# A sigmoid gate's logits and exponential in a gated mix of sliding-window attention and a GEGLU layer

## The chip, the cores and the metric

The kernel runs on one core of a Trainium2 chip. The time is device microseconds (us) of one execution. The median of 7 runs of the kernel before is 740.52 us, the lowest 739.31 and the highest 741.72. Engines are named as in the profile: PE is TensorE (matmuls), PEld its weight loads, DVE is VectorE, ACT is ScalarE, POOL is GpSimd, SP is SyncE, which issues most of the DMAs here.

## What is computed

With x of 2048 rows by 1024 columns, the output is `g * a + (1 - g) * b`, where

```
g = sigmoid((x * gate_w).sum(-1, keepdims=True))      # one number per row
a = attention(x @ wqkv) @ wo                          # 32 heads of 32, window of 8 keys, dilation 2
b = (gelu(x @ w_gate) * (x @ w_up)) @ w_down          # 1024 -> 3584 -> 1024
```

The attention of a row looks at the keys 0, 2, 4 ... 14 rows back, with a softmax over the 8. Everything stored is bfloat16.

## The kernel before

**Tiling.** The 2048 rows are worked on as four chunks of 512 rows (`SC`), two chunks forming a "super" step (`sup`). x stands transposed in `xr`, two chunks at a time, eight tiles of 128 columns (`KT`) per chunk; `xT(c, kt)` is one such tile, 128 by 512. The projections q, k, v of chunks 0 and 1 are plain products (`qkv`, `qkv_outer`, matmuls at L469). Those of chunks 2 and 3 (`qkv_pair`, L585), the GEGLU layer (`ffn`, L952) and the output products (`down`, L1096) use a Strassen scheme with seven block products. Its sums of blocks ("forms") are made on DVE: of x in `x_forms` (L449 to L454, called T1, T2, T3, T4 below, in the order of the code), of the q, k, v weights in `qkv_forms` (L552), of the GEGLU weights in `wforms` (L430). T3 is made in place over a tile of x, so it waits for the gate's matmuls of the even chunk (key `("z", c0)`) to have read that tile.

**Attention** is done on DVE and ACT alone, in halves of 256 rows: `scores` (products and sums, L765, L771), then `att_half`: transposes (L828), folds (L835, L838), maximum (L851), subtraction (L858), the exponential on ACT (L863), sums, the reciprocal (L869), the multiplication by the gate (L871), and the weighting of v (L904 to L921).

**The gate.** `gate(c)` multiplies chunk c's eight x tiles with the gate vector `gcol`. It uses the 128x128 array as four column tiles of 32: the eight tiles go in two rounds of four, each round's four matmuls to different groups of 32 output partitions (L693). The output bank thus holds four partial sums in four groups of 32 equal rows. DVE transposes the bank in blocks of 32 (L699) and copies the 16 columns that matter into `zq` (L703). Later `gate_sum(c)` adds the four partial sums with four small float32 matmuls against the 0/1 matrix `qsum` (L717), and DVE clamps the result to +-80 into `zc` (L721). `gate_exp(c)` takes the exponential on ACT into `ez` (L728), and `gate_tail(c)` makes `1/(1+ez)` on DVE in `omg` (L737 to L740). The output products are scaled by `omg` when they leave PSUM; the attention weights are multiplied by `ez`.

**Order.** Eight generators (`main`, `loads`, `wforms`, `x_forms`, `qkv_forms`, `preps`, `attention`, `scores`) yield operations with an engine, a cost in us and dependencies. The planner `Weave.run` holds the head of each generator and always emits the one whose planned start plus the generator's bias is smallest (0.0 for `main` and `loads`, 0.1 for the forms, 0.3 for `attention`, 0.5 for `scores`). The emitted order is final for each engine; the chip follows it and waits where data are not there. A changed cost in the planner can therefore change the order on any engine. Within one generator the order is that of the code. `gate(0)` is issued after chunk 0's projections, `gate_sum(0)` in chunk 1's, `gate(1)` before the first GEGLU, `gate_sum(1)` two steps into it. `gate(2)` and `gate(3)` come after the first output products and before `qkv_pair(2)`, with both sums behind it. `gate_exp(c)` comes in the attention stream, after the subtraction of the chunk's first half and before its exponential, but waits only for `zc`. An ACT operation has a table name; where it differs from the last one (exponential or gelu), the planner adds 1.29 us, and the chip runs an ACT_TABLE_LOAD.

**Setup.** `ident`, the identity for the transposes of x, lies in a corner of `hT`, a large tile that later takes other data. `qsum` is built on POOL with a memset and four affine selects.

Of the kernel before, what the change touches and what calls it, by code (L numbers as in the profile page):

```python
# [8 lines left out]
ACT = mybir.ActivationFunctionType  # L9
ALU = mybir.AluOpType  # L10
BF16 = mybir.dt.bfloat16
F32 = mybir.dt.float32
AP = bass.AP

P = 128
# [4 lines left out]
SC = 512  # L20
NST = SC // P
# [3 lines left out]
ZMAX = 80.0  # L25
# [111 lines left out]
def kernel(  # L137
# [12 lines left out]
    nc = tc.nc  # L150
    Bsz, S, D = A_x.shape
    Df = B_w_gate.shape[1]
    x = A_x.rearrange("b s d -> (b s) d")
    o2 = out.rearrange("b s d -> (b s) d")
    assert Bsz == 1
    KT = D // P
# [18 lines left out]
    scale = float(DH) ** -0.5  # L175
# [3 lines left out]
    consts = ctx.enter_context(tc.tile_pool(name="consts", bufs=1))  # L179
    persist = ctx.enter_context(tc.tile_pool(name="persist", bufs=1))  # L180
    work = ctx.enter_context(tc.tile_pool(name="work", bufs=2))
    small = ctx.enter_context(tc.tile_pool(name="small", bufs=1))
# [8 lines left out]
    hT = persist.tile([P, 2 * NST, FT, P], BF16)  # L191
# [7 lines left out]
    banks = [psum.tile([P, SC], F32, name=f"ps{i}") for i in range(8)]  # L199
    xbuf = persist.tile([P, NB, NWIN * AC], BF16)  # L200
    gcol = consts.tile([P, KT], BF16)
    ident = hT[:, NST + 1, 0, :]
    w = Weave(nc, tc)
    n = NWIN * AC
    V = nc.vector.tensor_tensor
# [1 line left out]
    def xT(c, kt):  # L207
        return xr[:, 2 * (c % 2) + kt // KH, kt % KH, :]

    def hflat(j, f0, n):  # L210
        return hT[:, j, f0:f0 + n, :].rearrange("p f s -> p (f s)")
# [4 lines left out]
    def dve(cost, fn, deps=(), **kw):  # L216
        return Op("DVE", cost, fn, deps, **kw)

    def act(cost, fn, deps=(), **kw):
        return Op("ACT", cost, fn, deps, **kw)  # L220

    def pe(n, fn, deps=(), **kw):
        return Op("PE", n * MM, fn, deps, tail=0.17, **kw)
# [3 lines left out]
    def bank_take():  # L227
        best = min(range(len(bank_free)), key=lambda i: -1.0 if bank_free[i][1] is None else bank_free[i][1].end)
        return bank_free.pop(best)

    def bank_give(i, op):
        bank_free.append((i, op))
# [41 lines left out]
        nc.tensor.matmul(banks[7][:], lhsT=warm[:, 0:P], rhs=warm, start=True, stop=True)  # L274
    wj = consts.tile([P, 1], F32)
    nc.scalar.activation(out=wj[:], in_=warm[:, 0:1], func=ACT.Exp)
    make_identity(nc, ident)
    qsum = consts.tile([P, 32], F32)
    nc.gpsimd.memset(qsum[:], 0.0)
    for d in range(-P + 32, 1, 32):  # L280
        nc.gpsimd.affine_select(out=qsum[:], in_=qsum[:], compare_op=ALU.not_equal, fill=1.0, base=d,
                                pattern=[[-1, 32]], channel_multiplier=1)
    nc.vector.memset(kT[0][:, :, 0:HALO], 0.0)
    nc.vector.memset(vT[0][:, :, 0:HALO], 0.0)
    with nc.allow_non_contiguous_dma(reason="gate vector, one element per partition"):
# [170 lines left out]
    gates = {}  # L456
# [227 lines left out]

    def gate(c):
        i, free = bank_take()
        dx = [("x", c, kt) for kt in range(KT)] if c else []

        def go():
            for r in range(KT // 4):  # L690
                for q in range(4):
                    kt = 4 * r + q
                    nc.tensor.matmul(banks[i][32 * q:32 * (q + 1), :], lhsT=gcol[:, kt:kt + 1].to_broadcast([P, 32]),  # L693
                                     rhs=xT(c, kt), start=(r == 0), stop=(r == KT // 4 - 1),
                                     tile_position=(0, 32 * q), skip_group_check=True)
        o = pe(KT // 4 + 1, go, ([free] if free else []) + dx, key=("z", c))
        yield o
        zt = work.tile([P, SC], F32, tag="u2", bufs=2, name="zt")
        e = dve(0.63, lambda: nc.vector.transpose(out=zt[:], in_=banks[i][:]), [o])  # L699
        yield e  # L700
        bank_give(i, e)
        zq = small.tile([P, SC // 32], F32, tag="zq", bufs=2, name="zq")
        e = dve(0.1, lambda: nc.vector.tensor_copy(out=zq[:], in_=zt[:].rearrange("p (b j) -> p b j", j=32)[:, :, 0]), [e],  # L703
                key=("zq", c))
        yield e
        zc = small.tile([P, SC // 32], F32, tag="zc", bufs=2, name="zc")
        ez = small.tile([P, SC // 32], F32, tag="ez", bufs=2, name="ez")
        omg = small.tile([P, NST], F32, tag="omg", bufs=3, name="omg")
        gates[c] = (ez, omg, zc, zq)

    def gate_sum(c):
        i, free = bank_take()
        zc, zq = gates[c][2:]

        def go():
            for q in range(4):
                nc.tensor.matmul(banks[i][32 * q:32 * (q + 1), 0:SC // 32], lhsT=qsum[:], rhs=zq[:], start=True, stop=True,  # L717
                                 tile_position=(0, 32 * q), skip_group_check=True)
        o = pe(1, go, [("zq", c)] + ([free] if free else []))
        yield o  # L720
        e = dve(0.1, lambda: nc.vector.tensor_scalar(out=zc[:], in0=banks[i][:, 0:SC // 32], scalar1=ZMAX, scalar2=-ZMAX,  # L721
                                                     op0=ALU.min, op1=ALU.max), [o], key=("zc", c))
        yield e
        bank_give(i, e)

    def gate_exp(c):
        ez, zc = gates[c][0], gates[c][2]
        e = act(0.1, lambda: nc.scalar.activation(out=ez[:], in_=zc[:], func=ACT.Exp), [("zc", c)], table="exp", lag=1.0,  # L728
                key=("ez", c))
        yield e  # L730

    def gate_tail(c):
        ez, omg = gates[c][:2]

        def tail():
            og = small.tile([P, SC // 32], F32, tag="og", name="og")
            nc.vector.tensor_scalar(out=og[:], in0=ez[:], scalar1=1.0, scalar2=1.0, op0=ALU.mult, op1=ALU.add)  # L737
            nc.vector.reciprocal(out=og[:], in_=og[:])
            for q in range(4):
                nc.vector.tensor_copy(out=omg[32 * q:32 * (q + 1), :],  # L740
                                      in_=og[32 * q:32 * (q + 1), :].rearrange("p (j q) -> p j q", q=4)[:, :, q])
        yield dve(1.2, tail, [("ez", c)], lag=0.6, key=("omg", c))
# [59 lines left out]
    def att_half(c, a, h):  # L802
# [13 lines left out]
        def lsb():  # L816
            return flat("z").bitcast(F32)[:, 0:CW].rearrange("p (w c) -> p w c", w=NWIN)
# [40 lines left out]
        o = dve(tt(CW, True), lambda: V(out=lsb(), in0=lsb(), in1=m4()[:, 0:1, :].to_broadcast([P, NWIN, CB]),  # L858
                                        op=ALU.subtract), [o])
        yield o  # L860
        if a == 0:
            yield from gate_exp(c)
        e = act(0.55, lambda: nc.scalar.activation(out=lsb(), in_=lsb(), func=ACT.Exp, scale=scale), [o], table="exp",  # L863
                lag=0.6)
        yield e
        if a == 0:
            yield from gate_tail(c)
# [74 lines left out]
            if t + 2 == NT:  # L942
                xb_give(box["ab"], ms[t + 1])

    def ffn(sup, mid, early=()):
        T3, B22, B11, B21 = xr[:, 0], xr[:, 1], xr[:, 2], xr[:, 3]
        T1, T2, T4 = tf[:, 0], tf[:, 1], tf[:, 2]

# [26 lines left out]
        for i in range(FT + 2):  # L975
# [6 lines left out]
                yield ev[f, "seed"]  # L982
            while late:
                yield late.pop(0)
            if i == 1:
                for g in early:
                    yield from g
            if i >= FT:
                yield from mid[i - FT]
            if i >= 2:  # L990
# [191 lines left out]
    def main():  # L1182
        ne = 0
        for j in range(NST):
            for k0 in range(0, KT, KH):
                i, free = bank_take()
                pt = banks[i][:].bitcast(BF16)[:, 0:KH * P].rearrange("p (k s) -> p k s", k=KH)

                def go(pt=pt, j=j, k0=k0):
                    for kk in range(KH):  # L1190
                        nc.tensor.transpose(out=pt[:, kk, :], in_=hflat(j, k0 + kk, 1), identity=ident)
                o = Op("PE", 0.3, go, [free] if free else [], tail=0.17)
                yield o
                dst = xr[:, k0 // KH, :, j * P:(j + 1) * P]
                if ne % 2:
                    e = act(0.48, lambda pt=pt, dst=dst: nc.scalar.copy(out=dst, in_=pt), [o], key=("pt", j, k0 // KH))
                else:
                    e = dve(0.34, lambda pt=pt, dst=dst: nc.vector.tensor_copy(out=dst, in_=pt), [o],
                            key=("pt", j, k0 // KH))
                yield e  # L1200
                bank_give(i, e)
                ne += 1
        yield from qkv_outer(0)
        yield from qkv(0, 1)
        yield from qkv(0, 2)
        yield from gate(0)
        yield from halo(1)
        for which in range(3):
            yield from qkv(1, which)
            if which == 0:  # L1210
                yield from gate_sum(0)
        yield from gate(1)
        for sup in range(NSUP):
            c0 = 2 * sup
            more = sup + 1 < NSUP
            parts = down(c0)
            yield from ffn(sup, parts, [gate_sum(1)] if sup == 0 else [])
            yield from parts[2]
            if more:
                yield from halo(c0 + 2)  # L1220
                yield from gate(c0 + 2)
                yield from gate(c0 + 3)
                yield from qkv_pair(c0 + 2)
                yield from gate_sum(c0 + 2)
                yield from gate_sum(c0 + 3)
                yield from halo(c0 + 3)
            for part in down(c0 + 1):
                yield from part
            if more:
                yield from q_move(c0 + 3)  # L1230
# [33 lines left out]
```

## Time and profile before

| what | value |
|---|---|
| median of the runs | 740.52 us |
| the profiled execution's own time | 741.35 us |
| its span on the core | 739.6 us |
| mean granted PE clock | 0.992 |
| PE busy | 721.5 us (98%) |
| DVE busy | 631.2 us (85%) |
| ACT busy | 312.5 us (42%) |
| L693, gate matmuls | 32, in four groups of 8 |
| L717, matmuls of the partial sums | 32 records, 8 per chunk |
| L728, gate exponentials | 4, 0.22 us each |
| ACT_TABLE_LOAD | 11 in all, 1.283 us each |

The span is what the profiler saw of the core; the execution's own time is 1.75 us longer. A matmul's duration in a group (379 ns) is its passage through the array; in a dense stretch matmuls start every 0.219 us (49 in 10.74 us). Sums of PE durations are therefore no measure of PE's time; gaps and the chain are.

### The profile page before, as it was taken

How to read it: one execution, taken by the hardware profiler on the slowest of the kernel's cores; microseconds unless marked ns; L12 is line 12 of the kernel's file. 1: busy time of each engine (PE TensorE's matmuls, PEld its weight loads, DVE VectorE, ACT ScalarE, POOL GpSimd, SP SyncE). 2: the span in 40 equal slices, each digit the busy share in tenths (PEclk: the TensorE clock that was granted, in tenths of full speed). 3: DMA queues.
4: the chain of work that ended last, by engine and by line, in shares of the span. 5: the costliest groups of instructions: out<-in, count | busy, mean ns of one | idle time of the engine just before them, and what ended most of it. 6: DMA issues, size and time to landing. Idle time of an engine off the chain costs nothing.

```text
span 739.6 us, 9888 instructions
## 1 busy us (share of the span) xinstructions
PE 721.5 (98%) x3330; PEld 355.7 (48%) x3397; DVE 631.2 (85%) x935; ACT 312.5 (42%) x530; POOL 72.0 (10%) x128
## 2 busy tenths in 40 slices
PE   8999999999999999969999999999999999999997
PEld 5666644444444444425665444444444444444443
DVE  2689999999999999996999999989999999896300
ACT  2333455558555542015444122585558554310110
POOL 2234422121111000000000001000000000001000
PEclk9999999999999999979999999999999999999999
DMA  8999955555646469960235999746464645899992
GB/s 306 316 326 361 388 195 178 163 179 164 196 146 205 158 197 323 318 224 28 86 115 167 313 310 319 242 144 172 129 178 133 172 138 162 275 308 326 335 302 103
DMA packets 150435, 162.68 MB, mean 220 GB/s; under 512 B 22896, under 2 KB 110960, under 8 KB 150384
## 3 DMA queue, kind: packets, MB, share of 16 engines
q1 hardware_dynamic: 141552, 134.25, 59.0%
q0 software_dynamic: 8544, 27.27, 10.1%
q8 instruction: 26, 0.43, 0.3%
q10 hardware_dynamic: 288, 0.52, 0.2%
q14 instruction: 25, 0.20, 0.1%
HBM read 129.50 MB, written 28.31 MB: 213 GB/s over the span
## 4 chain that ended last, share of the span: by engine, by line
PE 92%; DMA 6%; issue 1%; DVE 1%; SPq 0%; ACT 0%; DVEq 0%
PE ps L952 46%; PE ps L1096 27%; PE ps L585 10%; PE ps L469 9%; DMA ring<-in_A_wqkv_dram 3%; DMA ring<-oforms 1%; DMA ring<-in_A_wo_dram 1%; DMA hT<-in_B_w_down_dram 1%; SPq L302 0%; DVE zt L699 0%; DVE tf L451 0%; DVE tf L449 0%; PE ps L693 0%; SPq L270 0%; DVE ring L552 0%
## 5 line engine op out<-in xcount | busy, mean ns | idle before, releaser
L952 PEld LDWEIGHTS <-ring 128*128 128x128 bf16 x1568 | 153.2, 98 | 185.0 <-issue 0.4
L952 PE MATMUL ps<-xr,ring 128*128 128x512 bf16 x878 | 210.4, 379 | 0.9
L952 PE MATMUL ps<-tf,ring 128*128 128x512 bf16 x658 | 162.6, 379 | 0.8
L1096 PE MATMUL ps<-ring,hT 128*128 128x512 bf16 x693 | 159.7, 379 | 0.8
L1096 PEld LDWEIGHTS <-hT 128*128 128x128 bf16 x708 | 69.2, 98 | 83.4
L765 DVE TENSOR_TENSOR xbuf<-qo,kT 128x2048 bf16<-128x2048 bf16 x64 | 77.4, 1217 | 2.9 <-ACT kT L491 2.9
L904 DVE TENSOR_TENSOR xbuf<-xbuf,vT 128x2048 bf16<-128x2048 bf16 x64 | 77.3, 1216 | 0.1
L771 DVE TENSOR_TENSOR xbuf<-xbuf 128x2048 bf16<-128x2048 bf16 x56 | 68.1, 1216 | 0.1
L585 PEld LDWEIGHTS <-ring 128*128 128x128 bf16 x336 | 44.1, 132 | 39.2 <-DVE ring L552 9.7
L1131 ACT ACTIVATE ost<-ps,omg 128x512 bf16<-128x512 f32 x16 | 11.0, 687 | 113.4 <-PE ps L1096 110.2
L469 PE MATMUL ps<-xr,ring 128*128 128x512 bf16 x250 | 55.7, 380 | 0.9 <-DMA ring<-in_A_wqkv_dram 0.6
L1024 ACT ACTIVATE gl<-ps 128x512 bf16<-128x512 f32 x56 | 33.5, 597 | 51.7 <-PE ps L952 51.2
L981 ACT COPY ps<-ps 128x512 f32<-128x512 f32 x56 | 32.0, 571 | 55.1 <-PE ps L952 54.9
L1123 POOL DMA_DIRECT2D out_dram<-ost x24 | 13.0, 540 | 433.9 <-ACT ost L1131 340.2
L1096 PE MATMUL ps<-ring,qo 128*128 128x512 bf16 x187 | 49.0, 379 | 1.0 <-DMA ring<-in_A_wo_dram 0.5
L469 PEld LDWEIGHTS <-ring 128*128 128x128 bf16 x256 | 36.4, 144 | 19.7 <-DMA ring<-in_A_wqkv_dram 1.4
L996 DVE TENSOR_TENSOR hT<-hT,gl 128x1024 bf16<-128x1024 bf16 x56 | 38.4, 685 | 8.7 <-ACT hT L993 7.6
L585 PE MATMUL ps<-xr,ring 128*128 128x512 bf16 x187 | 43.0, 379 | 0.4 <-issue 0.2
L585 PE MATMUL ps<-tf,ring 128*128 128x512 bf16 x142 | 36.2, 403 | 7.3 <-DVE ring L552 7.2
L1036 DVE TENSOR_TENSOR u<-ps,u 128x512 f32<-128x512 f32 x56 | 38.3, 685 | 5.3 <-PE ps L952 4.3
L912 DVE TENSOR_TENSOR xbuf<-xbuf 128x1024 bf16<-128x1024 bf16 x64 | 41.9, 685 | 0.6
L438 POOL DMA_DIRECT2D fforms<-ring x56 | 30.5, 544 | 119.7 <-DVE ring L430 116.5
(106 smaller groups left out, 727.1 us busy)
## 6 DMA issues: line engine op xcount, KB each, us to landing
ring<-dforms SPq DMA_DIRECT2D x112, 256.0 KB, 4.8
ring<-in_B_w_down_dram SPq DMA_DIRECT2D x84, 256.0 KB, 4.3
ring<-in_B_w_gate_dram SPq DMA_DIRECT2D x56, 256.0 KB, 5.1
fforms<-ring POOLq DMA_DIRECT2D x56, 256.0 KB, 4.4
ring<-fforms SPq DMA_DIRECT2D x56, 256.0 KB, 3.9
ring<-in_B_w_up_dram SPq DMA_DIRECT2D x42, 256.0 KB, 3.7
ring<-in_A_wqkv_dram SPq DMA_DIRECT2D x40, 256.0 KB, 5.9
ring<-oforms SPq DMA_DIRECT2D x32, 256.0 KB, 5.6
```

The lines of the kernel that those rows point to most:

```text
L469: nc.tensor.matmul(banks[bk][:], lhsT=lhsT, rhs=xT(c, kt), start=(kt == 0), stop=(kt == KT - 1))
L585: nc.tensor.matmul(banks[bk][:], lhsT=lhsT, rhs=rhs[:, kt, :], start=(start and kt == 0), stop=(kt == KH - 1), skip_group_check=True)
L765: V(out=w3(box[t]), in0=q_b, in1=k_w, op=ALU.mult)
L771: V(out=w3(box[0]), in0=w3(box[0]), in1=w3(box[t]), op=ALU.add)
L904: return dve(tt(n), taking(("p", t), lambda: V(out=w3(box["p", t]), in0=w3(box["ab"]), in1=v_w, op=ALU.mult)), [("qkv", c, 2, t), abo] + ( ...
L912: V(out=s4(t)[:, t % 2], in0=w3(box["p", t])[:, 0:4], in1=w3(box["p", t])[:, 4:8], op=ALU.add)
L952: nc.tensor.matmul(banks[bk][:], lhsT=wv[:, k, fl * P:(fl + 1) * P], rhs=rhs[:, k, :], start=(start and k == 0), stop=(k == KH - 1), skip_ ...
L981: ev[f, "seed"] = act(0.5, lambda f=f: nc.scalar.copy(out=banks[Bk[f]][:], in_=banks[A[f]][:]), [o, fr] if fr else [o])
L996: yield dve(tt(2 * SC), lambda f=f: nc.vector.tensor_tensor(out=hT[:, :, f, :], in0=hT[:, :, f, :], in1=gl[f][:].rearrange("p (j s) -> p j ...
L1024: nc.scalar.activation(out=gl[f][:, SC:2 * SC], in_=banks[A[f]][:], func=ACT.Gelu_apprx_tanh)
L1036: e = dve(tt(SC, True), lambda f=f: nc.vector.tensor_tensor(out=u2[f][:], in0=banks[Dk[f]][:], in1=u2[f][:], op=ALU.add), [o, ev[f, "u2"]])
L1096: nc.tensor.matmul(banks[bk][:], lhsT=l, rhs=wv[:, i, :], start=(start and k == 0), stop=(q == last and i == 1), skip_group_check=True)
```

## The change

The gate goes through the full array: eight matmuls per chunk, each with the gate vector broadcast over all 128 columns, accumulate into one bank, which then holds the finished sum in all rows. `qsum`, `zq` and `gate_sum` are gone, with the hook in `ffn` and the calls in `main`; DVE clamps `zt` straight into `zc`, inside `gate`. `gate_exp` is gone too: where a chunk's first half takes its exponential, one ACT operation issues the gate's exponential and the attention's, one behind the other; it waits for both the subtraction and `zc`. `ident` gets a tile of its own. The planner's cost of `gate` goes from 3 matmul times to 8; the operation of the two exponentials costs 0.65 in place of 0.1 and 0.55, and the gate's own `lag` of 1.0 is gone.

```diff
-    ident = hT[:, NST + 1, 0, :]
+    ident = consts.tile([P, P], BF16)
...
-    qsum = consts.tile([P, 32], F32)
-    nc.gpsimd.memset(qsum[:], 0.0)
-    for d in range(-P + 32, 1, 32):
-        nc.gpsimd.affine_select(out=qsum[:], in_=qsum[:], compare_op=ALU.not_equal, fill=1.0, base=d,
-                                pattern=[[-1, 32]], channel_multiplier=1)
...
     def gate(c):
         i, free = bank_take()
         def go():
-            for r in range(KT // 4):
-                for q in range(4):
-                    kt = 4 * r + q
-                    nc.tensor.matmul(banks[i][32 * q:32 * (q + 1), :], lhsT=gcol[:, kt:kt + 1].to_broadcast([P, 32]),
-                                     rhs=xT(c, kt), start=(r == 0), stop=(r == KT // 4 - 1),
-                                     tile_position=(0, 32 * q), skip_group_check=True)
-        o = pe(KT // 4 + 1, go, ([free] if free else []) + dx, key=("z", c))
+            for kt in range(KT):
+                nc.tensor.matmul(banks[i][:], lhsT=gcol[:, kt:kt + 1].to_broadcast([P, P]), rhs=xT(c, kt),
+                                 start=(kt == 0), stop=(kt == KT - 1))
+        o = pe(KT, go, ([free] if free else []) + ([("x", c, kt) for kt in range(KT)] if c else []), key=("z", c))
         yield o
         zt = work.tile([P, SC], F32, tag="u2", bufs=2, name="zt")
         e = dve(0.63, lambda: nc.vector.transpose(out=zt[:], in_=banks[i][:]), [o])
         yield e
         bank_give(i, e)
-        zq = small.tile([P, SC // 32], F32, tag="zq", bufs=2, name="zq")
-        e = dve(0.1, lambda: nc.vector.tensor_copy(out=zq[:], in_=...), [e], key=("zq", c))
-        yield e
+        yield dve(0.1, lambda: nc.vector.tensor_scalar(out=zc[:], in0=..., scalar1=ZMAX, scalar2=-ZMAX, ...), key=("zc", c))
...
-    def gate_sum(c):
-        ...
-    def gate_exp(c):
-        ez, zc = gates[c][0], gates[c][2]
-        e = act(0.1, lambda: nc.scalar.activation(out=ez[:], in_=zc[:], func=ACT.Exp), [("zc", c)], table="exp", lag=1.0,
-                key=("ez", c))
-        yield e
...
-        if a == 0:
-            yield from gate_exp(c)
-        e = act(0.55, lambda: nc.scalar.activation(out=lsb(), in_=lsb(), func=ACT.Exp, scale=scale), [o], table="exp",
-                lag=0.6)
+        def exps():
+            if a == 0:
+                nc.scalar.activation(out=gates[c][0][:], in_=gates[c][2][:], func=ACT.Exp)
+            nc.scalar.activation(out=lsb(), in_=lsb(), func=ACT.Exp, scale=scale)
+        e = act(0.65 if a == 0 else 0.55, exps, [o] + ([("zc", c)] if a == 0 else []), table="exp", lag=0.6,
+                key=("ez", c) if a == 0 else None)
         yield e
```

More of the change, by code (lines that the diff above doesn't have):

```diff
@@ L276 @@
     nc.scalar.activation(out=wj[:], in_=warm[:, 0:1], func=ACT.Exp)
-    make_identity(nc, ident)
-    qsum = consts.tile([P, 32], F32)
-    nc.gpsimd.memset(qsum[:], 0.0)
-    for d in range(-P + 32, 1, 32):
-        nc.gpsimd.affine_select(out=qsum[:], in_=qsum[:], compare_op=ALU.not_equal, fill=1.0, base=d,
-                                pattern=[[-1, 32]], channel_multiplier=1)
+    make_identity(nc, ident[:])
     nc.vector.memset(kT[0][:, :, 0:HALO], 0.0)
@@ L686, in gate @@
         i, free = bank_take()
-        dx = [("x", c, kt) for kt in range(KT)] if c else []
         def go():
-            for r in range(KT // 4):
-                for q in range(4):
-                    kt = 4 * r + q
-                    nc.tensor.matmul(banks[i][32 * q:32 * (q + 1), :], lhsT=gcol[:, kt:kt + 1].to_broadcast([P, 32]),
-                                     rhs=xT(c, kt), start=(r == 0), stop=(r == KT // 4 - 1),
-                                     tile_position=(0, 32 * q), skip_group_check=True)
-        o = pe(KT // 4 + 1, go, ([free] if free else []) + dx, key=("z", c))
+            for kt in range(KT):
+                nc.tensor.matmul(banks[i][:], lhsT=gcol[:, kt:kt + 1].to_broadcast([P, P]), rhs=xT(c, kt),
+                                 start=(kt == 0), stop=(kt == KT - 1))
+        o = pe(KT, go, ([free] if free else []) + ([("x", c, kt) for kt in range(KT)] if c else []), key=("z", c))
         yield o
@@ L701, in gate @@
         bank_give(i, e)
-        zq = small.tile([P, SC // 32], F32, tag="zq", bufs=2, name="zq")
-        e = dve(0.1, lambda: nc.vector.tensor_copy(out=zq[:], in_=zt[:].rearrange("p (b j) -> p b j", j=32)[:, :, 0]), [e],
-                key=("zq", c))
-        yield e
         zc = small.tile([P, SC // 32], F32, tag="zc", bufs=2, name="zc")
+        yield dve(0.1, lambda: nc.vector.tensor_scalar(out=zc[:], in0=zt[:].rearrange("p (b j) -> p b j", j=32)[:, :, 0],
+                                                       scalar1=ZMAX, scalar2=-ZMAX, op0=ALU.min, op1=ALU.max),
+                  key=("zc", c))
         ez = small.tile([P, SC // 32], F32, tag="ez", bufs=2, name="ez")
         omg = small.tile([P, NST], F32, tag="omg", bufs=3, name="omg")
-        gates[c] = (ez, omg, zc, zq)
-    def gate_sum(c):
[L712 to L722, printed above, removed]
-        yield e
-        bank_give(i, e)
-    def gate_exp(c):
-        ez, zc = gates[c][0], gates[c][2]
-        e = act(0.1, lambda: nc.scalar.activation(out=ez[:], in_=zc[:], func=ACT.Exp), [("zc", c)], table="exp", lag=1.0,
-                key=("ez", c))
-        yield e
+        gates[c] = (ez, omg, zc)
     def gate_tail(c):
-        ez, omg = gates[c][:2]
+        ez, omg, zc = gates[c]
         def tail():
@@ L943, in att_half, with ffn @@
                 xb_give(box["ab"], ms[t + 1])
-    def ffn(sup, mid, early=()):
+    def ffn(sup, mid):
         T3, B22, B11, B21 = xr[:, 0], xr[:, 1], xr[:, 2], xr[:, 3]
@@ L984, in ffn @@
                 yield late.pop(0)
-            if i == 1:
-                for g in early:
-                    yield from g
             if i >= FT:
@@ L1190, in go @@
                     for kk in range(KH):
-                        nc.tensor.transpose(out=pt[:, kk, :], in_=hflat(j, k0 + kk, 1), identity=ident)
+                        nc.tensor.transpose(out=pt[:, kk, :], in_=hflat(j, k0 + kk, 1), identity=ident[:])
                 o = Op("PE", 0.3, go, [free] if free else [], tail=0.17)
@@ L1209, in main @@
             yield from qkv(1, which)
-            if which == 0:
-                yield from gate_sum(0)
         yield from gate(1)
@@ L1216, in main @@
             parts = down(c0)
-            yield from ffn(sup, parts, [gate_sum(1)] if sup == 0 else [])
+            yield from ffn(sup, parts)
             yield from parts[2]
@@ L1223, in main @@
                 yield from qkv_pair(c0 + 2)
-                yield from gate_sum(c0 + 2)
-                yield from gate_sum(c0 + 3)
                 yield from halo(c0 + 3)
```

## The prediction

> **What bounds the kernel now.** I read the page's slices first, then the chain of waits, then the timelines where the chain leaves PE. The slices:
>
> ```profile
> PE   8999999999999999969999999999999999999997
> PEclk9999999999999999979999999999999999999999
> ```
>
> PE is full from slice 1 on but for slice 17, and only there does its clock fall. The chain shows that the gate lies in the full parts:
>
> ```profile
> 50.32 0.55 PE ps L693 x8
> ...
> 64.76 0.26 PE ps L717 x8
> ...
> 92.80 0.55 PE ps L693 x8
> ...
> 98.64 0.19 PE ps L717 x8
> ...
> 103.94 10.74 PE ps L952 x49
> ...
> 403.06 0.25 PE ps L717 x16
> ```
>
> Columns are start, length, what. Chunk 0's and 1's gates (L693) and all partial sums (L717) stand between matmuls that follow without a gap; 49 matmuls in 10.74 us make 0.2192 us each. The gates of chunks 2 and 3 are not on the chain. PE's timeline around the hole of slice 17:
>
> ```profile
> 318.72 1.05 PE L693 MATMUL ps<-xr,gcol 128*32 128x512 bf16 x16
> 319.97 1.67 PE L585 MATMUL ps<-xr,ring 128*128 128x512 bf16 x7 [0.21 <-issue]
> 323.19 0.41 PE L585 MATMUL ps<-tf,ring 128*128 128x512 bf16 x1 [1.54 <-DVE ring L552]
> 325.26 0.62 PE L585 MATMUL ps<-tf,ring 128*128 128x512 bf16 x1 [1.66 <-DVE ring L552]
> 329.82 5.89 PE L585 MATMUL ps<-tf,ring 128*128 128x512 bf16 x14 [3.95 <-DVE ring L552]
> ```
>
> After both gates PE has one burst, then idles 1.54 + 1.66 + 3.95 = 7.15 us for weight forms of L552. The last row has 14 matmuls in 5.7 us: windows of 1 us show a granted clock of 0.50 from 326 to 335. At full clock they take 14 x 0.2192 = 3.07, so the slow clock costs 2.7 us. DVE meanwhile (five of its rows):
>
> ```profile
> 319.37 2.31 DVE L828 STREAM_TRANSPOSE xbuf<-xbuf 128x2048 bf16<-128x2048 bf16 x1
> 321.61 1.18 DVE L449 TENSOR_TENSOR tf<-xr 128x2048 bf16<-128x2048 bf16 x1
> ...
> 325.72 0.71 DVE L699 STREAM_TRANSPOSE zt<-ps 128x512 f32<-128x512 f32 x1
> ...
> 327.54 0.70 DVE L699 STREAM_TRANSPOSE zt<-ps 128x512 f32<-128x512 f32 x1
> ...
> 329.35 4.78 DVE L552 TENSOR_TENSOR ring<-ring 128x512 bf16<-128x512 bf16 x14
> ```
>
> DVE never rests there: attention, four x forms, the gates' transposes, and only then the forms that PE wants. So one price list holds where PE is full and another in the hole.
>
> **The change part by part.**
>
> Gates of chunks 0 and 1: each goes from 0.55 us to 8 x 0.2192 = 1.75, +1.20, and nothing hides it: 2 x 1.20 = +2.41.
>
> Partial sums of chunks 0 and 1: 0.26 + 0.19 = 0.45 us leave the full part; those of 2 and 3, 0.25 more, leave at 403. Sum -0.70.
>
> Does the +1.96 before the hole reach its end? DVE sets that end, and DVE is held to PE: in the GEGLU stage L1036 waited for PE 16 times (4.3 us) and L1015 18 times (3.9 us), the last such wait being 0.48 us at 260.5. From there DVE works densely to 329. A later PE moves that anchor, and so the hole's end. I take the whole 1.96; the lower end is 0, if DVE had slack unseen.
>
> Gates of chunks 2 and 3: also +2.41 on PE, but ahead of 7.15 us of idling. The first burst would end near 324 instead of 321.6 on the old axis, and the form it meets is at 323.2. I take 0. The cover gone, they cost +2.41. Below nothing: the planner sees these gates 5 matmul times later each (1.08), and may put forms ahead of the transposes and T3. If the 14 forms of L552 went first, where T3 (L453) starts now at 326.35, the 3.95 us wait would shrink by 3.0 (329.35 less 326.35) and the slow clock's 2.7 could go with it: -5.7. The nearest rows are those of today's order, so I keep 0.
>
> The slow clock stays in my sum, since the 3.95 us wait is still there. The Trainium skill ("TensorE: Matmul & The Clock Gate", Part 1) says that the clock falls to half after an idle window of some 3.4 us, windows running free of the kernel. The row agrees in kind: the fall came about 325, after 3.2 us of broken idling since 321.6. By the rule a gate that fills 2.4 us of the idling could put the fall off, for -2.7 at most; with a wait of 3.95 still whole it should fall anyway.
>
> DVE: a gate loses the copy L703 (0.16) and the clamp L721 (0.17) and gains a clamp from SBUF, put at 0.16 by L703. In the hole one replaces the other: 0. The clamps at 403 lie beside dense PE: 0.
>
> ACT: the gate's exponential (0.22) moves from before to beside the attention's. What the step waits for is late already: the subtraction L858. Chunk 3 is the case in the middle of the GEGLU, where gelus have to wait for a table:
>
> ```profile
> 556.87 1.28 ACT L728 ACT_TABLE_LOAD   x1
> 558.17 0.22 ACT L728 ACTIVATE ez<-zc 128x16 f32<-128x16 f32 x1
> ...
> 559.38 0.63 ACT L863 ACTIVATE xbuf<-xbuf 128x512 f32<-128x512 f32 x1
> 560.03 1.28 ACT L1040 ACT_TABLE_LOAD   x1
> ...
> 562.33 0.59 ACT L1006 COPY m<-ps 128x512 f32<-128x512 f32 x1
> ```
>
> Merged, load and both exponentials are one block of 1.28 + 0.22 + 0.63 = 2.1 us at about 559.4. Queued behind it are a gelu L1040, L993 and the copy L1006, for which PE waits before the block's fourth product. L1006 normally starts at 554.53 plus the step of 6.04, 560.57; here it ended at 562.92, and PE wanted it near 563.15: the gelu L1024 started at 556.26 on its product's end, the next product ends four matmuls later at 557.1, and one step on that is 563.15. So 0.24 us are left; 1.5 us more (the load and the exponential shifted behind it) would stall PE by 1.2. The plain block at 172.28 (load, exponential, then L1006 ended 174.69, wanted near 174.95) passed with 0.26 to spare, and the merged step adds 0.22. I take 0, with ends 0 and +1.2.
>
> Tables: no load disappears, since each gate exponential already shares its load with the attention's (261.85 and 556.87) or finds it there (74.32). The Trainium skill ("ScalarE: Activation LUTs", Table sets) advises to do calls of one set together, at an estimated 2.66 us for each switch saved. By it the sum would be 2.66 lower if one were saved; the eleven loads give no candidate.
>
> POOL and SP: five POOL instructions for `qsum` (0.12 and 1.06 us, done by 3.75 us) stand behind the identity and before nothing that PE awaits: 0. They uncover at most 1.2 at the start, where DMA leads the chain until 24. No DMA is added. Loads that were put down to L717 (SP waited 0.5 and 0.4) find the matmul before it instead. A bank is held 1.2 us longer by a gate and not taken by a sum: 0. `ident` on its own: 0, as the load into its old place waits for the same transposes of x.
>
> Sum: 2.41 - 0.45 - 0.25 = +1.71. Against the profiled execution: 741.35 + 1.71 = 743.06. That one stands 0.83 above the median, 740.52, from which I forecast 742.2.
>
> **The rivals.**
>
> The hole shrinks. For it: the gates' transposes and T4 stand before the awaited L552, and both come later in the plan. Against it: these generators have the smaller bias or come first in a tie. At its price, 740.52 + 1.71 - 5.7 = 736.5. This is the other side; it decides once the hole loses 3.2 us (1.71 + 1.48).
>
> The early gates are hidden. If DVE runs free of PE before the hole, only -0.25 is left: 740.3. For it: DVE dense from 271 to 334. Against: its waits for PE until 260.5.
>
> The hole or ACT grows. If both late gates come out in full, 1.71 + 2.41: 744.6; the stall of 1.2 on top gives 745.8. For it: 0.24 us of slack at L1006, and free planner time before later transposes that attention operations (bias 0.3) can fill, L828 with its 2.3 us above all.
>
> That the change doesn't do what it says: exponentials that are not adjacent. It would show on ACT and move nothing by itself.
>
> **How the numbers follow.** A measurement of this kernel tells about 0.2%, 1.48 us: slower is above 742.0, faster below 739.04. The forecast has 0.45, the growing hole or ACT stall 0.23, the shrinking hole 0.20, the hidden gates 0.12. The growing case is slower throughout; the forecast lies 0.2 over the bound, but its open ends (ACT's 1.2, part of 2.41) point upward: 0.37 slower and 0.08 same. The shrinking case I put at 0.18 faster and 0.02 same, the hidden gates at 0.02 faster and 0.10 same. That makes slower 0.60, same 0.20, faster 0.20. The range takes the priced ends, 736.5 to 745.8; the forecast's own is 741.4 to 743.4 (a third of the late gates' 2.41 less, or the stall of 1.2 more).
>
> **What would show it.** Right: L693 as two pieces of 1.75 us at about 50 and 94 on the chain, no L717; the GEGLU's first matmul at 95.5 for 93.34 (two gates more, one sum of 0.26 less: +2.15); sixteen gate matmuls in 3.5 us near 321; waits for L552 of some 5 us, the clock at 0.5 for some 10 us; eleven table loads. Wrong: another order of L828, L699, L453, L454 and L552 on DVE around 320 to 333, or a gap on PE before the L952 that waits for L1006 near 563. An order changed elsewhere, where no gap is today, would only add.

## The result and the profile after

The changed kernel takes 742.78 us (median of 16 runs, 741.52 to 743.93), the kernel before 740.53 (38 runs). The ratio is 1.0029, with a 95% interval of 1.0021 to 1.0036: 2.25 us slower, where 1.71 were forecast (742.2). The first profiled execution of the changed kernel took 741.72 us, 1.06 under its median; a second one (run e12 below) took 743.54. Both are used here, since they differ in two places that the change has nothing to do with. All ratios leave out runs that lie far above the others of the same kernel; that concerned one run, of 1557.78 us, in e7.

The slices of the changed kernel's page, then its chain at the same places as before (start, length, what):

```profile
PE   8999999999999999969999999999999999999997
PEclk9999999999999999989999999999999999999999
```

```profile
49.55 1.73 PE ps L685 x8
...
92.72 1.73 PE ps L685 x8
...
97.31 10.82 PE ps L923 x49
```

The line numbers have moved: L685 is the gate, L923 the GEGLU, L464 the first projections, L580 and L547 the later ones and their weight forms, L1064 the output products, L797 the attention's transpose (before: L693, L952, L469, L585, L552, L1096, L828). The early gates are 1.73 us each for 0.55, still in the full part; the partial sums are gone. The hole of slice 17 on PE, and some of DVE's rows beside it:

```profile
319.11 3.62 PE L685 MATMUL ps<-xr,gcol 128*128 128x512 bf16 x16
322.56 1.89 PE L580 MATMUL ps<-xr,ring 128*128 128x512 bf16 x8
324.29 0.38 PE L580 MATMUL ps<-tf,ring 128*128 128x512 bf16 x1
326.04 0.41 PE L580 MATMUL ps<-tf,ring 128*128 128x512 bf16 x1 [1.37 <-DVE ring L547]
327.53 0.41 PE L580 MATMUL ps<-tf,ring 128*128 128x512 bf16 x1 [1.08 <-DVE ring L547]
332.21 4.12 PE L580 MATMUL ps<-tf,ring 128*128 128x512 bf16 x12 [4.27 <-DVE ring L547]
```

```profile
320.16 2.31 DVE L797 STREAM_TRANSPOSE xbuf<-xbuf 128x2048 bf16<-128x2048 bf16 x1
322.39 1.18 DVE L444 TENSOR_TENSOR tf<-xr 128x2048 bf16<-128x2048 bf16 x1
...
326.62 0.42 DVE L820 TENSOR_TENSOR xbuf<-xbuf 128x256 f32<-128x256 f32 x1
327.05 0.43 DVE L547 TENSOR_TENSOR ring<-ring 128x512 bf16<-128x512 bf16 x1
327.39 0.71 DVE L690 STREAM_TRANSPOSE zt<-ps 128x512 f32<-128x512 f32 x1
...
331.32 4.44 DVE L547 TENSOR_TENSOR ring<-ring 128x512 bf16<-128x512 bf16 x13
```

The last wait is shorter than this row says. The trace lacks the record of the first matmul behind it; its weight load is there:

```profile
331.80 0.15 PEld L580 LDWEIGHTS <-ring 128*128 128x128 bf16 x2 [4.16 <-DVE ring L547]
```

In the kernel before, and in e5, the first weight load behind the wait and its matmul start within 0.01 us of each other, so the long wait ends at 331.80 and lasts 3.86 us, not 4.27. The second execution (e12) lacks the same record: its wait ends at 332.77, not 333.18, and lasts 3.86 us too. The numbers below use the weight loads here. PE's waits for forms are then 6.3 us for 7.15; the 2.4 us that the late gates got longer have filled idle time. But the long wait ends at 331.80 for 329.82, of which 0.8 us is the later start of the output products. On DVE the gates' transposes have moved behind one attention operation (L820) and one more weight form (L547), as the planner now thinks the gates later.

Cut at six moments that exist in every kernel here, the timelines give these stretches (us; "long wait" is the last wait for the weight forms, and its end the start of the matmuls behind it):

| stretch | before | after | e12 | e3 | e5 | e10 |
|---|---|---|---|---|---|---|
| start to first gate | 50.25 | 49.38 | 50.42 | 49.43 | 50.27 | 49.55 |
| to second gate | 42.47 | 43.17 | 43.16 | 43.16 | 43.17 | 42.48 |
| to first output product | 167.49 | 168.44 | 168.36 | 168.54 | 168.36 | 167.91 |
| to end of long wait | 69.61 | 70.81 | 70.83 | 69.08 | 70.83 | 69.64 |
| to second output products | 73.42 | 71.70 | 72.58 | 72.54 | 70.17 | 70.85 |
| to last matmuls | 331.53 | 331.62 | 331.62 | 331.61 | 331.62 | 331.54 |

The second row is the same within 0.01 us in all executions of one kind of gate. By the second and third rows the early gates and sums cost 0.70 + 0.87 = 1.6 us (e12 against before). The third row varies more: e10, which does the same work as the kernel before up to there, has 167.91, 0.28 of it a wait for ACT, and against it the cost would be 1.15. The fourth row is DVE's: 1.2 us more. The fifth gives back 0.84 (e12) to 1.7 (after). The first row moves by 1 us between two executions of one kernel (49.38 and 50.42).

### The profile page after: what moved, and what is told of

It is laid out like the page before. It is cut to its first block, busy times and chain, and to the rows that moved or that the text cites. A ratio compares the mean times of both kernels' runs of the same rounds, so it can differ in the third digit from the quotient of the medians.

```text
span 739.9 us, 9811 instructions
## 1 busy us (share of the span) xinstructions
PE 722.9 (98%) x3298; PEld 358.0 (48%) x3365; DVE 631.1 (85%) x931; ACT 312.3 (42%) x530; POOL 71.2 (10%) x123
## 4 chain that ended last, share of the span: by engine, by line
PE 92%; DMA 4%; DVE 2%; issue 1%; ACT 0%; ACTq 0%
PE ps L923 45%; PE ps L1064 25%; PE ps L464 11%; PE ps L580 10%; DMA ring<-oforms 1%; DMA ring<-in_A_wo_dram 1%; DMA ring<-in_A_wqkv_dram 1%; DMA ring<-fforms 1%; DMA ring<-dforms 1%; DMA hT<-in_A_x_dram 0%; PE ps L685 0%; DVE hT L1032 0%; PE ps L1159 0%; DVE tf L1032 0%; DVE ring L547 0%
## 5 line engine op out<-in xcount | busy, mean ns | idle before, releaser
L923 PEld LDWEIGHTS <-ring 128*128 128x128 bf16 x1568 | 153.4, 98 | 185.2 <-issue 0.4
L923 PE MATMUL ps<-xr,ring 128*128 128x512 bf16 x878 | 210.4, 379 | 0.8
L923 PE MATMUL ps<-tf,ring 128*128 128x512 bf16 x659 | 162.6, 379 | 0.8
L1064 PE MATMUL ps<-ring,hT 128*128 128x512 bf16 x693 | 159.4, 379 | 0.7
L1064 PEld LDWEIGHTS <-hT 128*128 128x128 bf16 x708 | 69.3, 98 | 83.5
L580 PEld LDWEIGHTS <-ring 128*128 128x128 bf16 x336 | 44.0, 131 | 37.0 <-DVE ring L547 8.5
L464 PE MATMUL ps<-xr,ring 128*128 128x512 bf16 x250 | 55.3, 379 | 0.6 <-DVE xr L1166 0.3
L952 ACT COPY ps<-ps 128x512 f32<-128x512 f32 x56 | 32.0, 572 | 55.7 <-PE ps L923 55.6
L1064 PE MATMUL ps<-ring,qo 128*128 128x512 bf16 x189 | 49.1, 379 | 1.0 <-DMA ring<-in_A_wo_dram 0.4
L464 PEld LDWEIGHTS <-ring 128*128 128x128 bf16 x256 | 36.7, 143 | 18.8 <-DMA ring<-in_A_wqkv_dram 0.3
L580 PE MATMUL ps<-xr,ring 128*128 128x512 bf16 x188 | 43.2, 379 | 0.3
L983 DVE TENSOR_TENSOR hT<-ps,m 128x512 bf16<-128x512 f32 x56 | 38.4, 686 | 4.2 <-PE ps L923 3.9
```

The lines of the kernel that those rows point to most:

```text
L464: nc.tensor.matmul(banks[bk][:], lhsT=lhsT, rhs=xT(c, kt), start=(kt == 0), stop=(kt == KT - 1))
L580: nc.tensor.matmul(banks[bk][:], lhsT=lhsT, rhs=rhs[:, kt, :], start=(start and kt == 0), stop=(kt == KH - 1), skip_group_check=True)
L923: nc.tensor.matmul(banks[bk][:], lhsT=wv[:, k, fl * P:(fl + 1) * P], rhs=rhs[:, k, :], start=(start and k == 0), stop=(k == KH - 1), skip_ ...
L983: ev[f, "up2"] = dve(tt(SC, True), lambda f=f: nc.vector.tensor_tensor(out=hs(f, 1), in0=v3(banks[Bk[f]][:]), in1=v3(m5[f][:]), op=ALU.add ...
L1064: nc.tensor.matmul(banks[bk][:], lhsT=l, rhs=wv[:, i, :], start=(start and k == 0), stop=(q == last and i == 1), skip_group_check=True)
```

## The experiments

The theory after the result: PE's time for the early gates sets the difference, and what the plan does to DVE's order in the hole comes on top. The rivals: the joint issue of the exponentials costs it, or the early gates are hidden behind DVE. Later runs ask what the hole itself costs.

**e1: full-array gates, separate exponentials.** The changed kernel with this put back, and `gate_exp` defined as before:

```diff
-        e = act(0.65 if a == 0 else 0.55, exps, [o] + ([("zc", c)] if a == 0 else []), table="exp", lag=0.6,
-                key=("ez", c) if a == 0 else None)
+        if a == 0:
+            yield from gate_exp(c)
+        e = act(0.55, lambda: nc.scalar.activation(out=lsb(), in_=lsb(), func=ACT.Exp, scale=scale), [o], table="exp",
+                lag=0.6)
```

> The gate goes through the full array as in the changed kernel, but its exponential stays an ACT operation of its own, as in the kernel before. Theory (the gates' matmuls in the full stretch of PE set the difference): as the changed kernel, 742.8 us (742.0 to 743.6). Rival (the joint issue of the exponentials costs the time): back at the time before, 740.5 us.

Measured: 740.99 us, 1.0008 of the kernel before on the same chip (0.9999 to 1.0017). Taken alone that speaks for the rival. The profile says otherwise: the early gates cost the same (43.17 between the two gates), and the exponential on its own does harm, in the way that the prediction feared from the joint one. PE's waits in e1:

```profile
PE ps L927 <- ACT m L978: 3.1, 2, 1.5
PE ps L580 <- DVE ring L547: 2.0, 1, 2.0
```

and ACT's rows before the first of the two stalls (PE resumes at 261.80):

```profile
254.92 1.28 ACT L703 ACT_TABLE_LOAD   x1
256.21 0.22 ACT L703 ACTIVATE ez<-zc 128x16 f32<-128x16 f32 x1
...
256.93 1.28 ACT L1012 ACT_TABLE_LOAD   x1
258.23 0.63 ACT L1012 ACTIVATE gl<-u 128x512 bf16<-128x512 f32 x1
...
259.35 1.28 ACT L838 ACT_TABLE_LOAD   x1
260.64 0.63 ACT L838 ACTIVATE xbuf<-xbuf 128x512 f32<-128x512 f32 x1
261.18 0.57 ACT L978 COPY m<-ps 128x512 f32<-128x512 f32 x1
```

A gelu has come between the two exponentials. e1 has 18 table loads, the kernels before and after 11, and the copy L978 comes 1.53 us too late for PE, twice. These 3.1 us were won back in the hole: another DVE order leaves one wait of 2.0 us there, and in the profiled execution the clock stays at 1.000 (mean granted, 0.995 in the changed kernel). Of the twelve runs six are like it, at 1.000 and 739.82 to 740.90 us; the six others have 0.997 or 0.998 and 741.07 to 742.73 us. So e1 doesn't isolate the joint issue, because the plan changes elsewhere with it.

**e2: column tiles, joint exponentials.** The same edit in the other direction, in the kernel before.

> The other half alone: four column tiles and partial sums as before, but the two exponentials issued together. Theory: as before, 740.5 us (739.7 to 741.3). Rival (the joint issue costs): 742.8 us. A stall of PE behind a table load in the middle of the GEGLU would show as up to 1.2 us more.

Measured: 740.50 us, 1.0000 (0.9991 to 1.0008), PE's waits for forms 6.9 us. PE waits for no ACT operation in its trace, so the joint block holds up nothing: that rival falls. The ratio is a net one, though. Here too the planner has ordered DVE anew: two more attention operations come before the first x form, and the long wait ends 68.77 us after the first output product, for 69.61 before.

**e3: the planner told the old cost.**

```diff
-        o = pe(KT, go, ...)
+        o = pe(KT // 4 + 1, go, ...)
```

> The changed kernel, but the planner is told the old cost of a gate, 3 matmul times in place of 8. The chip's work is that of the changed kernel. Theory: 742.8 us within 0.8. Rival (the later gates in the plan change the order on DVE, and that costs the time): 740.5 us.

Measured: 740.54 us, 1.0003 (0.9994 to 1.0011). A miss for the theory: with the same work on the chip most of the difference is gone. The early gates are still 1.7 us dearer (table), but DVE does two more attention operations (L804, L807) before the first x form (L444), with the gates' transposes next to each other, and the long wait ends 69.08 us after the first output product, not 70.81:

```profile
318.38 2.31 DVE L797 STREAM_TRANSPOSE xbuf<-xbuf 128x2048 bf16<-128x2048 bf16 x1
320.73 0.69 DVE L804 TENSOR_TENSOR xbuf<-xbuf 128x1024 bf16<-128x1024 bf16 x1
321.46 0.69 DVE L807 TENSOR_TENSOR xbuf<-xbuf 128x512 f32<-128x512 bf16 x1
322.07 1.22 DVE L444 TENSOR_TENSOR tf<-xr 128x2048 bf16<-128x2048 bf16 x1
...
325.80 0.71 DVE L690 STREAM_TRANSPOSE zt<-ps 128x512 f32<-128x512 f32 x1
326.54 0.17 DVE L694 TENSOR_SCALAR zc<-zt 128x16 f32<-128x16 f32 x1
326.63 0.71 DVE L690 STREAM_TRANSPOSE zt<-ps 128x512 f32<-128x512 f32 x1
```

What the slower PE work loses, the hole wins back: against the profile of before its end comes 0.5 us sooner and the stretch behind it is 0.9 us shorter. In the hole it is the order of e2, but for the transposes, and not that of the kernel before. The clock has a part in it: seven of eleven have a mean granted clock of 0.998, where the changed kernel has 0.992 to 0.995 in all its runs but one.

**e4: early gates twice.**

```diff
-            for kt in range(KT):
+            for kt in [k for _ in range(2 if c < 2 else 1) for k in range(KT)]:
```

> The changed kernel with the eight matmuls of the gates of chunks 0 and 1 issued twice (the second pass starts anew, so the sum is the same); the order of everything else is kept. Theory: 2 x 8 matmuls of 0.216 us on the path, +3.45 us over the changed kernel, 746.2 us. Rival (DVE runs free of PE before the hole, so early PE work is hidden): 742.8 us.

Measured: 745.83 us, 1.0074 (1.0062 to 1.0086) against 1.0029 for the changed kernel: 0.45% or 3.3 us more, for 3.45 us of matmuls. The stretches to the second gate and to the first output product are 44.90 and 170.08, 1.73 and 1.64 more. DVE's part follows: the long wait ends 70.81 us after the first output product, as in the changed kernel. PE time ahead of the hole arrives at the end almost whole; that it is hidden is refuted.

**e5: late gates twice.** As e4 with `c >= 2`.

> The changed kernel with the eight matmuls of the gates of chunks 2 and 3 issued twice; the order of everything else is kept. Theory: PE waits 6.7 us for weight forms right behind them, so the 3.46 us more are hidden: 742.8 us, and up to 1.4 us less if the shorter rest keeps PE's clock up longer. Rival (late gates come out in full): 746.2 us.

Measured: 740.99 us, 1.0012 (1.0004 to 1.0021): sixteen matmuls more, and 1.3 us by the ratios (1.8 by the medians) less than the changed kernel. PE's rows in the hole, and its clock (windows: stretch, length, busy PE, PEld, DVE, ACT, POOL, clock, DMA share, GB/s):

```profile
320.63 7.07 PE L685 MATMUL ps<-xr,gcol 128*128 128x512 bf16 x32
...
332.63 3.00 PE L580 MATMUL ps<-tf,ring 128*128 128x512 bf16 x13 [2.56 <-DVE ring L547]
```

```profile
328.00:330.00 2.00, 2.00 (x10) 1.02 (x8) 1.97 (x4) 1.11 (x2) 0.00 (x0) 1.00 0.02 7
330.00:332.00 2.00, 0.07 (x1) 0.00 (x0) 1.97 (x4) 0.03 (x1) 0.00 (x0) 1.00 0.00 0
332.00:334.00 2.00, 1.37 (x7) 0.76 (x8) 2.00 (x7) 0.60 (x2) 0.00 (x0) 1.00 0.00 0
```

The same stretches of the changed kernel, second execution:

```profile
328.00:330.00 2.00, 0.41 (x1) 0.11 (x1) 1.96 (x5) 0.00 (x0) 0.00 (x0) 1.00 0.03 11
330.00:332.00 2.00, 0.00 (x0) 0.00 (x0) 1.97 (x4) 0.00 (x0) 0.00 (x0) 0.72 0.00 0
332.00:334.00 2.00, 0.82 (x2) 0.45 (x4) 2.00 (x7) 0.52 (x1) 0.00 (x0) 0.50 0.00 0
334.00:336.00 2.00, 2.00 (x6) 0.76 (x5) 2.00 (x8) 0.66 (x2) 0.00 (x0) 0.50 0.00 0
```

The late gates are hidden, all 6.9 us of them. In the profiled execution PE, idle for 2.56 us in one piece in place of 6.3 in three, keeps its clock, and the stretch behind the long wait falls from 72.58 (e12) to 70.17. Not every run does: six of eleven have a mean clock of 0.999 or 1.000 and take 739.76 to 740.99 us, five have 0.997 or 0.998 and take 741.49 to 742.52.

**e6, e7, e8: the weight forms first.** The planner's biases of the forms, in the changed kernel (e6) and in the kernel before (e7, e8):

```diff
-    w.run([..., (0.1, x_forms()), (0.1, qkv_forms()), ...])
+    w.run([..., (0.1, x_forms()), (-0.4, qkv_forms()), ...])      # e6, e7
+    w.run([..., (-3, x_forms()), (-3, qkv_forms()), ...])         # e8
```

> The changed kernel with the planner's bias of the weight forms of q, k, v at -0.4 in place of 0.1. On DVE this puts the forms that PE waits for ahead of the second gate transpose, T3 and T4. Theory (DVE's order in the hole is the larger part of what the kernel can lose or win there): the last wait of 4.3 us shrinks to about 1 and the clock stays up, 742.8 - 3.0 - 1.4 to -2.7: 737.1 to 738.4 us. Rival (the hole is set by loads or by PE, not by this order): 742.8 us.

> The kernel before with the same bias of -0.4. On DVE the forms then stand behind one transpose of the gates only. Theory: the wait of 3.95 us shrinks by some 3 and the clock stays up, 740.5 - 3.0 - 2.0: 735.5 us; with e6 the difference of about 1.7 us between the two kinds of gate comes back, since neither has a hole to hide it. Rival: 740.5 us.

> The kernel before with a bias of -3 for the forms of x and for those of the q, k, v weights. On DVE T1 and the weight forms come ahead of the attention's transpose of 2.3 us. Theory: the hole closes nearly whole, 7.15 us of waits and 2.0 to 2.7 of slow clock less what the first forms still wait for their loads: 733 to 735 us. Rival (forms planned early stand before their data and hold up DVE): 740.5 us or more.

Measured: e6 742.26 us, 1.0029 (1.0017 to 1.0041); e7 1.0086 (1.0072 to 1.0100), some 6.4 us slower; e8 753.80 us, 1.0184 (1.0170 to 1.0198). All three theories fell. In the hole the edit did what it should: e6's waits for forms are down to 2.0 us and its clock is 1.000. But PE's waits in e6 and e8 show new ones, by another releaser:

```profile
PE ps L580 <- DVE vT L641: 2.9, 1, 2.9
PE ps L580 <- DVE ring L547: 2.0, 3, 0.8
PE ps L580 <- ACT hT L634: 1.3, 1, 1.3
```

```profile
PE ps L585 <- DVE vT L646: 13.6, 1, 13.6
PE ps L585 <- DVE ring L552: 2.0, 2, 1.6
```

The attention work that was put off stands later, as a dense block ahead of the sums (L646) that PE needs for v: PE resumes at 389.09 in e6 after 2.94 us, at 391.36 in e7 after 5.61, at 397.68 in e8 after 13.63. DVE works through the block without a rest (L904 and its neighbours from 376 to 395 in e8). In e8 the rival is right as well: the early forms hold up DVE, which waits 5.0 us for loads and 2.5 us for PE at L552, where the kernel before has no such wait. PE also waits for ACT in the GEGLU, 1.3 us in e7 and 3.0 us in e8. So the hole is one place where PE waits for a DVE that is full; each of these orders that emptied it moved the wait.

**e10: the kernel before, kept busy in the hole.**

```diff
         def go():
+            for kt in [k % KT for k in range(12 if c >= 2 else 0)]:
+                nc.tensor.matmul(banks[i][:], lhsT=gcol[:, kt:kt + 1].to_broadcast([P, P]), rhs=xT(c, kt),
+                                 start=True, stop=True)
             for r in range(KT // 4):
```

> The kernel before, with 12 needless full-array matmuls (their result is overwritten) ahead of the gate of chunk 2 and of chunk 3 each: 24 x 0.216 = 5.2 us of PE in the stretch where PE waits 7.15 us for weight forms. The order of everything else is kept. Theory (idling there costs a slow clock, and PE work there is free): no half clock, 740.2 less 2.0 to 2.7: 737.5 to 738.2 us. Rival (extra matmuls come out, or the clock falls all the same): 740.2 to 745.4 us.

Measured: 739.43 us, 0.9982 (0.9973 to 0.9992). It is the first of two versions that beat both kernels, by matmuls that compute nothing. The gain is 1.3 us by the ratio, less than expected. The runs show why: six of the twelve have a mean clock of 0.999 or 1.000 and take 737.75 to 739.30 us, the six others have 0.998 and take 739.57 to 741.42. So the matmuls spare the clock only in half of the runs; where the others lose it isn't on record. The profile is of the first kind: in it the long wait still ends when it did (69.64), is now 2.36 us, and the stretch behind it is 70.85 for 73.42.

```profile
324.84 1.95 PE L585 MATMUL ps<-xr,ring 128*128 128x512 bf16 x8
326.63 0.59 PE L585 MATMUL ps<-tf,ring 128*128 128x512 bf16 x2
329.58 3.33 PE L585 MATMUL ps<-tf,ring 128*128 128x512 bf16 x13 [2.36 <-DVE ring L552]
```

**e11: e3 and e5 together.**

> The changed kernel with the old planner cost of a gate (as in e3) and with the late gates' matmuls issued twice (as in e5). Theory: the two add up, 740.5 less 2.0: 738.5 us (737.8 to 739.2). Rival (both mend the same loss): 740.5 us.

Measured: 739.25 us, 0.9983 (0.9974 to 0.9992). The two add up, as e3's 1.0003 less what e5 saved would have it, though the median is 0.75 above the value expected. PE's one wait for forms is 1.5 us there, and all eleven runs have a mean clock of 0.999 or 1.000. It is as fast as e10, with the dearer early gates.

**e12: the changed kernel again.**

> The changed kernel as it is, beside these two on one chip, and a second profile of it, since the first lies 1.1 us under the median of its runs. Theory (the length of the slow clock after the hole differs from execution to execution): 742.8 us, and where this profile's time differs from 741.72, the difference stands between the first matmul after the long wait and the first of the second output products. Rival: it stands at the start, before 49 us.

Measured: 743.11 us, 1.0032 (1.0020 to 1.0044); the profiled execution 743.54. The 1.82 us between the two profiled executions stand in both places: 1.04 before the first gate, and 0.88 behind the long wait, where the 13 matmuls take 5.24 us (from 332.77 to 338.01) for 4.36 (from 331.80 to 336.16). Both are PE at half speed. At the start 125 matmuls from 7.99 took 28.77 us for 27.79: the first five start some 0.4 us apart, to 10.05, and those behind them 0.22, where in the first execution they start 0.22 us apart from 7.95 on. The granted clock has its first record at 10.02 in e12 and at 7.29 in the first execution, and is 1.00 from there to the hole. Behind the hole the clock is at 0.50 from 330.87 to 337.70, and from 328.14 to 334.96 in the first execution: equally long, but 4.9 us of it behind the wait against 3.2.

## Why the prediction was right, and where it was not

The direction, the size (2.25 for 1.71) and the main term were right; two terms that were put at 0 were not. That the sum came so near is partly luck: the early gates cost 0.4 less than forecast, the hole's end came 1.2 later, and a shorter slow clock gave back part of it. The sign that the prediction named as its own undoing, another order of these operations on DVE around 320 to 333, did appear.

*Gates of chunks 0 and 1, less their sums: forecast +1.96, measured +1.57.* It was mis-sized twice. 49 matmuls in 10.74 us leave out one that the chain booked as "issue": 50 in 10.79 make 0.2158 us, so a gate costs 1.73 and not 1.75. And the column tiles cost more than their rows show: between the two gates there are 192 other matmuls, 41.43 us, so before (42.47) gate and sum took 1.04 us where their rows say 0.55 + 0.26 = 0.81. After (43.17) it is 1.74, the eight matmuls.

*It reaches the end of the hole.* Right, by e4: 3.3 of 3.45 us.

*Gates of chunks 2 and 3 at 0.* Right for their matmuls: e5 doubles them and the time doesn't rise. The open question of this term was the order, which "I keep 0" left as today's. It changed against the kernel: the later gates let an attention operation and a weight form in ahead of the transposes, and the long wait ended 1.2 us later (fourth row). The rival "the hole grows" named this filling, though not its size. That the planner's cost decides the order is shown by e3, in which nothing else differs.

*The slow clock stays, at 2.7.* It stayed, but shorter: 6.82 us at half clock, where some 10 were expected. In the kernel before 14 matmuls behind the wait took 5.73 us, 2.7 too many; in the changed kernel 13 took 4.36 or 5.24, which is 1.6 or 2.4 too many. In these two profiles one matmul less behind the wait (0.2), the shorter loss (0.3 or 1.1) and the late sums (0.25) make up what the fifth row gives back. Part of that is no work of the change: the profile of before is of an execution with a long slow stretch, 10.24 us (325.07 to 335.31), where e2, with gates of the same kind, has 6.82. Of the 68 runs of the kernel before that stand beside the experiments, 42 have a mean clock of 0.994 or 0.995, as e2's profile, and 26 have 0.992 or 0.993, as the profile of before.

The rule quoted from the Trainium skill ("TensorE: Matmul & The Clock Gate", Part 1), of idle windows of some 3.4 us that run free of the kernel, fits the lengths: the slow stretches in the middle of the kernel last 6.82 or 6.83 us (after, e12, e2, e3, e4, and twice in e7), 10.24 (before) or 13.65 (e8), which is two, three and four times 3.41. The length of one wait doesn't decide it. In the kernel before the clock fell at 325.07, ahead of the wait of 3.95 us, as the prediction had read it; in e7 it fell with no wait over 1.64 us:

```profile
319.90 1.95 PE L585 MATMUL ps<-xr,ring 128*128 128x512 bf16 x8
323.48 0.41 PE L585 MATMUL ps<-tf,ring 128*128 128x512 bf16 x1 [1.64 <-DVE ring L552]
324.95 0.61 PE L585 MATMUL ps<-tf,ring 128*128 128x512 bf16 x1 [1.06 <-DVE ring L552]
```

```profile
322.00:324.00 2.00, 0.41 (x1) 0.11 (x1) 2.00 (x3) 0.46 (x1) 0.00 (x0) 1.00 1.07 412
324.00:326.00 2.00, 0.61 (x1) 0.11 (x1) 2.00 (x4) 0.00 (x0) 0.00 (x0) 0.56 0.56 215
326.00:328.00 2.00, 1.11 (x3) 0.34 (x4) 2.00 (x7) 0.00 (x0) 0.00 (x0) 0.50 0.02 6
```

The 3.41 us before that fall, at 324.22, hold some 1.4 us of matmuls. How much work a window may hold and still let the clock fall is not shown here. A single wait of 2.56 (e5), 2.36 (e10) or 2.0 us (e1) kept the clock in the profiled executions, and by the clocks above in about half of the runs; that fits windows whose place differs from run to run.

*Tables and the joint issue at 0.* Right: 11 loads before and after, and in e2 no wait of PE for ACT. The skill's advice to do calls of one set together ("ScalarE: Activation LUTs", Table sets) had no switch to save here, but e1 shows what it guards against, 18 loads. The price of 2.66 us for a switch, which the page gives under "What ACT_TABLE_LOAD costs", isn't borne out, and the measurement decides: in e1 a load takes 1.283 us, starts 0.01 us behind the copy before it (254.32 + 0.59, 254.92), and the exponential starts 0.01 us behind the load (254.92 + 1.28, 256.21).

*ACT's block in the GEGLU at 0, end +1.2.* Right in the changed kernel: PE nowhere waits for that copy. That the slack is thin shows in other orders: PE waits for it 1.29 us in e7 and e8, and 1.53 us a time in e1.

Put together, with e12 against the profile of before, whose difference of 2.19 us is near that of the medians: start +0.17, gates and sums +0.69 and +0.87, the hole's end +1.22, behind it -0.84, the rest +0.09, sum +2.20. The terms for the start and for the stretch behind the hole hold what the clock does in these two executions, and would be others in another pair.

## What to carry to other kernels

Price a change in PE work by the stretch it stands in: sixteen more matmuls cost 3.3 of their 3.45 us where PE is dense (e4), and less than nothing where it waits for DVE (e5). Where a planner orders the work, a changed cost is a change of its own; telling it the old cost shows what the order is worth (here about 2 us, 1.0029 less 1.0003), though the order that comes out need not be the one of the kernel before. One profile shows one execution: the granted clock of all runs tells whether it is a typical one. And a wait that is emptied by another order on a full engine comes back where the work that was put off stands.

## What the runs showed of the hardware

Matmuls without any use, issued into a wait of PE, made the kernel 0.18% faster (e10: 0.9982, 0.9973 to 0.9992): in the kernel before the granted clock fell to 0.50 in the middle of the idling (325.07) and came back only 10.24 us later, in the middle of the work behind the wait. In all traces that show such a fall inside the kernel it lasts two, three or four times 3.41 us. Four column tiles ran eight 128x512 matmuls in 0.55 us, but such a gate and its small sum cost 0.23 us beyond their own rows (42.47 us between the two early gates, and 42.48 in e10). And one kernel's executions differ by 1 us each at the start and behind the hole, by where the slow clock stands, so two profiles 0.4 us apart (741.35 and 741.72) stood for medians 2.25 us apart.
